# PSUM given out by the list of steps, singly or two banks side by side, in a Performer and Fourier-mixing kernel on one core

## The chip, the core and the metric

The kernel runs on one NeuronCore of a Trainium2 chip. The core has a matrix engine (TensorE, in the profile PE, with its weight loads shown apart as PEld), a vector engine (VectorE, DVE), a scalar engine (ScalarE, ACT), GpSimd (POOL) and a queue engine (SyncE, SP) that here only issues DMAs. Matrix products land in PSUM, eight banks of 512 float32 in each of 128 partitions. The metric is the device time of one execution in microseconds; a kernel's time is the median of several executions.

## The reference

Two blocks follow each other. The first is Performer attention on 8 batches of 8 heads with 576 rows of 64; the second a Fourier mixing with a two-layer perceptron on rows of 512:

```python
def phi(x):
    proj = np.einsum('bhsd,md->bhsm', x, omega)        # 64 -> 128 features
    h = proj - np.sum(x * x, axis=-1, keepdims=True) / 2.0
    h = h - np.max(h, axis=-1, keepdims=True)
    return np.exp(h) / np.sqrt(m)
q_p, k_p = phi(q * scale), phi(k * scale)
kv = einsum('bhsm,bhsd->bhmd', k_p, v); z = np.sum(k_p, axis=2)
x = einsum('bhsm,bhmd->bhsd', q_p, kv) / (einsum('bhsm,bhm->bhs', q_p, z)[..., None] + 1e-06)
# (B,H,S,D) -> (B,S,H*D), then
u = x + real(fft(fft(x, axis=1), axis=2))
un = (u - mean(u)) / sqrt(var(u) + 1e-06)
out = u + maximum(un @ w_ch1, 0.0) @ w_ch2             # 512 -> 2048 -> 512
```

q, k, v and omega are float32; the two weight matrices arrive as float64 and are narrowed on the chip.

## The kernel before

**Two halves.** The early half does attention, the mixing, the narrowing of the weights and the perceptron of four blocks of 128 rows ("plain"). The late half does the perceptron of the other eight blocks of 512 rows with Strassen's seven products (Winograd's form) for both layers: `first_of` for the first layer, `product_of` for the second.

**A list of steps.** The order of instructions on every engine is written out by the program itself. Each stream of work (a Python generator) yields a `Step` ahead of the instructions that it covers: engine or choice of engines, an assumed duration, the events that it needs, the buffers that it takes and gives back, and a `bias` in microseconds that is added to its start when steps are compared. `Listing.run` takes, again and again, the step with the earliest assumed start plus bias, and so fixes the order. A step marked `port` also needs an assumed port that DVE and POOL share; whoever is chosen for it holds that port. The order is then kept as it is; semaphores see to the data. Durations in the list steer the order alone.

**A pair of heads** (`attn(n)`, 32 of them, three under way at once). k and q of two heads are loaded side by side, turned by 9 transposes of 128 columns (line 396) and copied out by ACT. The projection `pairs_of` runs on nine columns of 128: twice four columns as quarters of the array (line 471, 64 by 64, four side by side, results in two banks), and the ninth as one product over the full array (line 461) against a matrix om2 that holds omega twice, with zeros beside it. `softmax` takes one bank at a time: DVE finds the negated maxima (line 412: 512 elements for a bank of a group of four columns, 256 for the ninth), ACT makes one exponential for each 128 (line 424). Then come kv (`kvp`, line 506, two banks, copied out by DVE or ACT in two instructions, lines 521 and 523), 9 transposes of q's features, and numerator and denominator (`ndp`, lines 550 and 558, two banks). Six DVE instructions divide them into x: two additions (571), a reciprocal (574) and three multiplications (581), of which the last covers 64 partitions.

**The mixing** (`mix`, once a batch) folds x on DVE or POOL (608 to 636), multiplies by cosine and sine tables (654, 681, 686), and `residual` adds the parts (700 to 717) and stores them.

**Weights.** 32 pieces of 512 KB are loaded on POOL's queue. For each, `narrow` makes a float32 out of the two halves of the float64: a first scaling on ACT or POOL (lines 333 and 331), four DVE instructions (335, 337, 340, 342) and a sum on POOL (344). After the last one, `w2_parts` makes sums of the second layer's weights (956), and `block_norms(0, ...)` prepares the first late block.

**PSUM.** Eight buffers of one bank come from a pool (`bank(name)`); the list counts free ones under the name "bank". The late half closes the early pools and opens a PSUM pool of its own.

**Late half.** `weight_sums` makes sums of the first layer's weights, 16 DVE instructions (line 1044) into w1s, a tile that lies where early tiles lay; `first_of` needs its first quarter for its second product. `loads_w2` reads pieces of the second layer's weights ahead of need into 15 buffers (line 1137).

## Time and profile before

| | us |
|---|---|
| runs, median of 4 (lowest to highest) | 1237.34 (1235.48 to 1239.09) |
| the profiled execution | 1239.09 |
| its span, first to last instruction | 1237.1 |
| PE busy in the span | 1201.9 |
| DVE busy | 770.2 |
| ACT busy | 456.1 |
| POOL busy | 393.6 |

The granted clock of TensorE was 0.992 in the mean. The early half's last product (line 886) runs until about 475 us and the late half's first one (line 1059) starts at 476.12. Busy time of PE counts every moment in which a product is in flight, so overlapping products are counted once and a busy PE is not yet one at its full rate. In a row of instructions the columns are the line, the engine and operation, the tiles written and read, the shapes and the count, then busy time and mean length in ns, and behind the next bar the engine's idle time ahead of them with what ended it.

### The profile page before, as it was taken

To read this page: it belongs to the slowest core of one execution; us is meant where nothing else is said; L and a number is where in the kernel's file an instruction comes from. 1 tells how busy PE (TensorE), PEld (TensorE's weight loads), DVE (VectorE), ACT (ScalarE), POOL (GpSimd) and SP (SyncE) were. 2 spreads that over 40 slices of the span, in tenths; PEclk is the share of its full clock that TensorE was granted. 3 is DMA by queue.
4 is the path that set the end of the run, shared out by engine and by line. 5 is a ranking of instruction groups with operands and counts; after the bars stand their busy time and mean duration, and the time that the engine had idled before them with its cause. 6 is when DMAs were issued, how large, how long until landed. Compare 5 with 4: busy or idle time off the path is not lost.

```text
span 1237.1 us, 31364 instructions
## 1 busy us (share of the span) xinstructions
PE 1201.9 (97%) x12513; PEld 1073.5 (87%) x12513; DVE 770.2 (62%) x1708; ACT 456.1 (37%) x1430; POOL 393.6 (32%) x462
## 2 busy tenths in 40 slices
PE   7999899999999998999999999999999999999997
PEld 5788878778887875899899899899899899899897
DVE  3999899997687625185185185276276276266265
ACT  5776666676664211222222222222222222222211
POOL 2544354643133110430430530530530530531430
PEclk8999999999999999999999999999999999999999
DMA  8555455646564345078078078078078068068155
GB/s 242 170 170 168 150 156 189 205 120 196 160 206 137 107 145 168 12 258 254 9 251 260 10 240 262 11 235 276 8 224 279 17 212 278 30 198 283 39 159 165
DMA packets 148736, 205.99 MB, mean 167 GB/s; under 512 B 49264, under 2 KB 62320, under 8 KB 148592
## 3 DMA queue, kind: packets, MB, share of 16 engines
q1 hardware_dynamic: 143984, 187.22, 48.2%
q0 software_dynamic: 4608, 16.78, 4.2%
q8 instruction: 99, 1.62, 0.5%
q14 instruction: 45, 0.37, 0.1%
HBM read 172.23 MB, written 35.91 MB: 168 GB/s over the span
## 4 chain that ended last, share of the span: by engine, by line
PE 85%; DVE 9%; ACT 3%; issue 1%; DMA 1%; SPq 0%; DVEq 0%; ACTq 0%
PE sx L1059 17%; PE sx L1204 16%; PE sz L1059 9%; PE sz L1204 8%; PE sy L1059 4%; PE hp L863 4%; PE sy L1204 4%; PE op L886 4%; PE yp L654 4%; PE tps L396 4%; PE pp L471 3%; ACT e L424 2%; PE kvp L506 2%; DVE nmx L412 2%; PE ndp L550 1%
## 5 line engine op out<-in xcount | busy, mean ns | idle before, releaser
L424 ACT ACTIVATE e<-pp,nmx 128x128 f32<-128x128 f32 x576 | 159.3, 407 | 46.4 <-DVE nmx L412 46.2
L1121 POOL TENSOR_TENSOR hs<-hid 128x256 f32<-128x256 f32 x64 | 46.5, 726 | 358.0 <-DVE hid L1047 358.0
L1047 DVE CUSTOM_DVE_ANT_0 hid<-sz,s 128x256 f32<-128x256 f32 x64 | 27.2, 425 | 182.4 <-PE sz L1059 174.5
L1059 PE MATMUL sx<-unT,w 128*128 128x256 f32 x512 | 127.7, 379 | 2.2 <-ACT s L1073 1.4
L1204 PE MATMUL sx<-wl,sums 128*128 128x128 f32 x896 | 115.4, 275 | 0.0
L1204 PE MATMUL sz<-wl,sums 128*128 128x128 f32 x896 | 114.2, 275 | 0.0
L412 DVE TENSOR_REDUCE nmx<-pp 128x4 f32<-128x512 f32 (+1 forms) x160 | 94.2, 628 | 30.8 <-PE pp L471 16.7
L1059 PEld LDWEIGHTS sx<-unT,w 128*128 128x128 f32 x512 | 96.6, 190 | 16.2 <-ACT s L1073 1.8
L1204 PEld LDWEIGHTS sz<-wl,sums 128*128 128x128 f32 x896 | 107.7, 192 | 0.4
L1204 PEld LDWEIGHTS sx<-wl,sums 128*128 128x128 f32 x896 | 107.6, 192 | 0.0
L1073 ACT ACTIVATE s<-sx 128x256 f32<-128x256 f32 x128 | 48.9, 383 | 152.3 <-PE sx L1059 74.3
L344 POOL TENSOR_TENSOR w<-w,raw 128x512 f32<-128x512 f32 x32 | 45.7, 1430 | 120.2 <-DVE raw L342 113.1
L1106 ACT ACTIVATE hid<-sx 128x256 f32<-128x256 f32 x64 | 24.5, 383 | 132.9 <-PE sx L1059 132.9
L471 PE MATMUL pp<-om,kqT 64*64 64x128 f32 x2048 | 71.1, 279 | 0.8 <-issue 0.6
L796 POOL TENSOR_TENSOR rstd<-rstd,mhalf 128x1 f32<-128x1 f32 x36 | 25.3, 702 | 142.9 <-DVE rstd L794 116.2
L471 PEld LDWEIGHTS pp<-om,kqT 64*64 64x64 f32 x2048 | 58.2, 136 | 12.2 <-issue 6.9
L1204 PE MATMUL sx<-wl,hid 128*128 128x128 f32 x512 | 67.6, 275 | 0.0
L863 PE MATMUL hp<-unT,w 128*128 128x128 f32 x512 | 62.2, 276 | 3.8 <-ACT e L424 2.8
L863 PEld LDWEIGHTS hp<-unT,w 128*128 128x128 f32 x512 | 59.5, 192 | 6.2 <-ACT e L424 3.4
L1059 PE MATMUL sx<-tt,w 128*128 128x256 f32 x256 | 64.2, 379 | 0.0
L1182 ACT ACTIVATE s<-sx 128x128 f32<-128x128 f32 x112 | 31.0, 277 | 88.5 <-PE sx L1204 60.7
L1059 PE MATMUL sz<-tt,w1s 128*128 128x256 f32 x256 | 61.9, 379 | 1.7 <-DVE w1s L1044 1.7
(134 smaller groups left out, 2578.5 us busy)
## 6 DMA issues: line engine op xcount, KB each, us to landing
wl<-w2l SPq DMA_DIRECT2D x392, 256.0 KB, 3.8
raw<-in_moe_w_ch_dram POOLq DMA_DIRECT2D x32, 512.0 KB, 4.7
kq<-in_k_dram SPq DMA_DIRECT2D x32, 288.0 KB, 3.6
kq<-in_q_dram SPq DMA_DIRECT2D x32, 288.0 KB, 4.8
vd<-in_v_dram SPq DMA_DIRECT2D x32, 288.0 KB, 4.5
out_dram<-ur SPq DMA_DIRECT2D x72, 128.0 KB, 3.0
u<-us SPq DMA_DIRECT2D x32, 256.0 KB, 4.4
ur<-us SPq DMA_DIRECT2D x32, 256.0 KB, 3.8
```

Of the source, the lines that this page charges most:

```text
L344: nc.gpsimd.tensor_tensor(out=dst, in0=dst, in1=lof, op=ALU.add)
L396: nc.tensor.transpose(ps[:, (j - j0) * 128 : (j - j0 + 1) * 128], src(j), ident[:])
L412: nc.vector.tensor_reduce(nmx[:, 0:num], ps[:, 0 : MF * num].rearrange("p (c m) -> p c m", m=MF), axis=AX.X, op=ALU.max, negate=True,)
L424: nc.scalar.activation(out=e[:, c, :], in_=ps[:, MF * c : MF * c + MF], func=AF.Exp, bias=nmx[:, c : c + 1],)
L471: nc.tensor.matmul(pps[c][cols, MF * m : MF * m + MF], lhsT=kqT[rows, j, cols], rhs=om2[rows, c, :],)
L654: nc.tensor.matmul(yp[:, 0:NK], lhsT=fold[:, c, n, :], rhs=tab[:, c, :], start=(c == 0), stop=(c == NC3 - 1),)
L863: nc.tensor.matmul(hp[:, 0:TP], lhsT=w1[:, dc, 128 * fc : 128 * fc + 128], rhs=unTs[key][:, dc, :], start=(dc == 0), stop=(dc == NDC - 1),)
L886: nc.tensor.matmul(yp[:, 0:DM], lhsT=hs[fc][:, 128 * i : 128 * i + 128], rhs=w2[:, fc, :], start=(fc == 0), stop=(fc == NFC - 1),)
L1059: nc.tensor.matmul(ps[:, 0:HT], lhsT=left(dc), rhs=right(dc), start=start and dc == 0, stop=(dc == D2 - 1), skip_group_check=True,)
L1073: nc.scalar.activation(out=s[:], in_=ps[:, 0:HT], func=AF.Copy)
L1121: nc.gpsimd.tensor_tensor(out=o, in0=l, in1=r, op=op)
L1204: nc.tensor.matmul(ps[:, 0:128], lhsT=left[:, f], rhs=wls[j, i, n][:, f], start=start and f == 0, stop=(f == 3), skip_group_check=True,)
```

## The change

PSUM becomes one tile of eight banks that lives through both halves. The list now keeps a time for each bank: a step takes a "bank" or a "duo", two neighbours that start at an even number, and `got()` hands the chosen banks to the code. A single bank is taken, where times are equal, from a pair that is half in use. What works on two banks at once in the new code: the maxima of a group of columns, the copy of kv, and the division in x. The ninth projection runs on quarters like the others and takes a duo; om2 has omega once. A step marked `port` holds the port only if its engine is DVE or POOL, and the first scaling in `narrow` is such a step, at 1.4 us for POOL where it was 1.0. The middle part of the second fold runs on DVE only. The first quarter of `weight_sums` moves into the early half and writes a tile of its own, with the third sum in that tile rather than in w1; the other three quarters stay. The v load of pair 0 joins the stream of the other v loads instead of following q of pair 0. The wl buffers go from 15 to 14. The memsets of om2 and of x's last rows go. Many biases and some assumed durations get other values.

```diff
+WIDTH = {"bank": 1, "duo": 2}
...
+    def on_port(self, eng):
+        return self.port and eng in (DVE, POOL)
...
+    def banks_at(self, n, t):
+        best = None
+        for i in range(0, 8, n):
+            free = self.banks[i] if n == 1 else max(self.banks[i], self.banks[i + 1])
+            key = (max(free, t), n == 1 and self.banks[i ^ 1] <= t, free, i)
+            if best is None or key < best:
+                best = key
+        return best[3], best[0]
...
-    NWL, NSUM = 15, 3
+    NWL, NSUM = 14, 3
...
-    psum = early.enter_context(tc.tile_pool(name="psum", bufs=8, space=PSUM))
+    psum = ctx.enter_context(tc.tile_pool(name="psum", bufs=1, space=PSUM))
+    banks = psum.tile([128, 8, 512], F32, name="banks")
...
+            yield Step(SP, 0.45, 3.6, makes=("kq", n), kb=288, bias=-2.98)
             nc.sync.dma_start(kq[:, R : 2 * R, :], q[b, h].rearrange(rows, r=R))
-            if n == 0:
-                yield from load_v(0)
...
-        yield Step(SP, 0.6, 4.0, take=(f"vd{n % NV}",), makes=("vd", n), kb=288)
+        yield Step(SP, 0.6, 4.0, take=(f"vd{n % NV}",), makes=("vd", n), kb=500, bias=0.52)
...
-        step = Step({ACT: 0.7, POOL: 1.0}, after=(("raw", i),), bias=0.22)
+        step = Step({ACT: 0.72, POOL: 1.4}, after=(("raw", i),), port=True, bias=1.11)
...
-        yield Step(DVE, 0.15 + 0.135 * num)
-        nmx = small.tile([P, 4], F32, name="nmx", tag="nmx", bufs=4)
+        yield Step(DVE, 0.15 + 0.27 * num, bias=-0.56)
+        nmx = small.tile([P, 2, 4], F32, name="nmx", tag="nmx", bufs=4)
+        pps = psum_of(b)
         nc.vector.tensor_reduce(
-            nmx[:, 0:num],
-            ps[:, 0 : MF * num].rearrange("p (c m) -> p c m", m=MF),
+            nmx[:, :, 0:num],
+            pps[:, :, 0 : MF * num].rearrange("p b (c m) -> p b c m", m=MF),
...
-            if len(ts) == 1:
-                nc.tensor.matmul(
-                    pps[0][:, 0 : 2 * MF],
-                    lhsT=kqT[:, js[0], :],
-                    rhs=om2[:].rearrange("p i m -> p (i m)"),
-                )
+            for m, j in enumerate(js):
+                for c, i in ((0, 0), (1, 1), (0, 1), (1, 0)):
+                    rows, cols = slice(D * c, D * c + D), slice(D * i, D * i + D)
+                    nc.tensor.matmul(
+                        pps[cols, c, MF * m : MF * m + MF],
+                        lhsT=kqT[rows, j, cols],
+                        rhs=om2[rows, :],
+                    )
...
+            if step.eng == DVE:
+                nc.vector.tensor_copy(out=kv[:], in_=kvp[:, :, 0 : D + 1])
+            else:
+                nc.scalar.activation(out=kv[:], in_=kvp[:, :, 0 : D + 1], func=AF.Copy)
...
+        nc.vector.tensor_scalar(rden[:], nd[:, :, :, D], DEN_EPS, None, op0=ALU.add)
         nc.vector.reciprocal(out=rden[:], in_=rden[:])
+        dst = x[:, :, 2 * D * pr : 2 * D * (pr + 1)].rearrange("p c (i d) -> p i c d", i=2)
+        nc.vector.tensor_tensor(
+            out=dst,
+            in0=nd[:, :, :, 0:D],
+            in1=rden[:].unsqueeze(3).to_broadcast([P, 2, 5, D]),
+            op=ALU.mult,
+        )
...
-            step = Step({DVE: 1.15, POOL: 2.5} if n else DVE, 1.15, port=True)
+            yield Step(DVE, 1.15, port=True, bias=-0.08)
...
+    w1s = [const.tile([128, 4, D2, GW], F32, name="w1s0")]
+    def weight_sums(groups):
+        yield Step(NONE, after=("converted",))
+        for g in groups:
...
+                if g == 0 and i == 2:
+                    o = w1s[0][:, 3]
...
-        + [w2_parts(), block_norms(0, mlpp), plain(), weights()]
+        + [w2_parts(), weight_sums((0,)), block_norms(0, mlpp), plain(), weights()]
...
-    psum = ctx.enter_context(tc.tile_pool(name="psum2", bufs=8, space=PSUM))
...
-    listing.run([late_norms(), halves(), loads_w2(), weight_sums()])
+    listing.run([late_norms(), halves(), loads_w2(), weight_sums((1, 2, 3))])
```

## The prediction

> **What bounds the kernel now.** I read the busy shares and the forty slices first, then the stretches of the early half, then the rows by shape, last the timeline where the halves meet. The page first:

> ```profile
> PE 1201.9 (97%) x12513; PEld 1073.5 (87%) x12513; DVE 770.2 (62%) x1708; ACT 456.1 (37%) x1430; POOL 393.6 (32%) x462
> ...
> PE   7999899999999998999999999999999999999997
> ...
> DVE  3999899997687625185185185276276276266265
> ```

> The reader should distrust the 62% of DVE: it is an average. From slice 2 to slice 9 DVE is as full as PE; from slice 17 on it is mostly free and PE alone is full. The change edits the first half, so that half is read by stretches (columns: PE, PEld, DVE, ACT, POOL busy, then clock, DMA share, GB/s):

> ```profile
> 31.00:279.00 248.00, 235.92 (x4428) 197.99 (x4417) 233.89 (x552) 170.98 (x573) 116.99 (x105) 0.99 0.55 165
> 279.00:403.00 124.00, 120.28 (x2224) 102.01 (x2223) 93.73 (x251) 76.64 (x253) 34.54 (x31) 1.00 0.56 174
> 403.00:475.00 72.00, 72.00 (x411) 52.33 (x409) 28.78 (x67) 13.98 (x43) 8.00 (x10) 1.00 0.32 108
> 475.00:500.00 25.00, 21.09 (x95) 17.70 (x95) 14.39 (x26) 5.00 (x14) 7.25 (x11) 1.00 0.63 211
> 0.00:31.00 31.00, 22.30 (x425) 18.06 (x428) 11.68 (x27) 17.75 (x57) 7.41 (x19) 0.89 0.83 242
> ```

> Between 31 and 279 us DVE works 233.9 of 248 us and PE 235.9. But PE's busy time holds overlaps: taking each matmul at its start-to-next-start time inside an unbroken group (0.112 us for 128 columns in full mode, 0.029 for a projection quarter, 0.429 for 512 columns) its work there is 207 us, so PE loses 41 us to waits and to changes of array shape, while DVE has 14 us left. DVE is the tighter of two tight engines. Between 279 and 403 the same sum gives PE 112 of 124; from 403 to 475 it has no gap at all, and behind 500 the slices show 9 throughout. So the change can earn before 403 and at the seam near 476, and nowhere else.

> **DVE over two banks.** The rows by shape, and one back-to-back series from the timeline (start, length):

> ```profile
> L412 DVE TENSOR_REDUCE nmx<-pp 128x4 f32<-128x512 f32 x128 | 82.3, 681 | 26.5 <-PE pp L471 16.7 <-ACT e L424 9.0 <-issue 0.6
> ...
> L581 DVE TENSOR_TENSOR x<-ndp,rden 128x256 f32<-128x256 f32 x64 | 24.2, 419 | 1.1
> ...
> L412 DVE TENSOR_REDUCE nmx<-pp 128x2 f32<-128x256 f32 x32 | 13.3, 416 | 4.3 <-ACT e L424 3.7 <-PE pp L461 0.4
> ```
> ```profile
> 113.97 2.46 DVE L412 TENSOR_REDUCE nmx<-pp 128x4 f32<-128x512 f32 x4
> ```

> The price of a reduction is not its 681 ns: four take 2.46 us, (2.46 - 0.68)/3 = 0.59 apart. The slope between the two shapes is (681-416)/256 = 1.035 ns an element, so 512 elements are 0.530 and what is paid per instruction is 0.068 us. Merging saves that and no element. Per pair of heads: two reductions go (four of 512 become two of 1024; the ninth stays one of 256), two of the three multiplications (256+256+128 becomes 640), one of the two additions into rden, and one copy of kv where DVE makes it (32 of 64 copies, so 0.5). That is 5.5 x 0.068 = 0.37 us, x 20 pairs (60 rows of L581 in that stretch, three a pair) = **7.5 us** of 233.9, and 11 pairs x 0.37 = 4 us up to 403, where DVE has room and it buys nothing. [...]

> **Conversion, port and POOL.** The weight conversion's three DVE lines are stretched:

> ```profile
> L335 DVE TENSOR_SCALAR raw<-raw x32: 407/422/1592, 28.9 to 264.9; 128x512 uint32<-128x512 uint32 x32
> L337 DVE SCALAR_TENSOR_TENSOR w<-w,raw x32: 673/682/1671, 29.4 to 274.7; 128x512 uint32<-128x512 uint32 x32
> L340 DVE TENSOR_SCALAR raw<-w x32: 427/429/1662, 30.1 to 275.4; 128x512 uint32<-128x512 uint32 x32
> ```

> In the stretch they take 20.35, 26.30 and 19.01 us for 31 each, 18.5 us above 31 medians. Their long ones are as long as a POOL operation (L331: 1.55), so DVE waits for POOL. The edit makes the list price L331 at 1.4 instead of 1.0 us on POOL, against 0.72 on ACT. ACT has 77 us idle in the stretch, so I take 12 of the 25 to move: 19 of POOL's 117 us, 16% of 18.5 = 3 us off DVE, for 8.5 us more on ACT. Ends: 0 (none move) and 18.5 (the new port order ends every clash). The middle fold now stays on DVE: POOL took one of 16, so DVE gains about 1.2 us of work. Net **2 us**; DVE in sum 9.5.

> **The ninth projection.** Line 461 takes 0.432 us at best from its start to the next group's, 0.536 in the median, because it lies in full mode beside quarters. A quarter group of four columns takes 0.924, so one is 0.231. Gain 0.20 to 0.31, I take 0.25: 5 us over 20 pairs, 2.9 over the 11 or 12 left. The new form has four maxima rather than two in that instruction, over the same 256 elements, and no more exponentials.

> Between 31 and 279 DVE falls by 9.5 and PE by 5; both are tight, so the stretch shrinks by something between: **7.5**. From 279 to 403 PE sets the pace: **2.5** of its 2.9.

> **The seam.** Columns: start, length, engine, then in brackets the idle time before and its releaser:

> ```profile
> 476.12 1.97 PE L1059 MATMUL sx<-unT,w 128*128 128x256 f32 x8 [0.87 <-DVE ur L899]
> 478.99 0.69 DVE L1044 TENSOR_TENSOR w1s<-w 128x512 f32<-128x512 f32 x1 [3.01 <-DMA out_dram<-ur]
> ...
> 479.78 1.97 PE L1059 MATMUL sz<-tt,w1s 128*128 128x256 f32 x8 [1.69 <-DVE w1s L1044]
> ...
> 490.00 1.13 PE L1059 MATMUL sx<-unT,w 128*128 128x256 f32 x4 [1.35 <-ACT s L1073]
> ```

> PE waits 0.87 for the old PSUM pool, 1.69 for sums that may not start until the last store has landed (their tile lies where the early tiles lay), and 1.35 behind sixteen sums on DVE. One PSUM tile ends the first; the first quarter of the sums, now made early in a tile of its own, ends the second: PE then has six products of 0.864 us to do before it needs a saved one, past 479.1. The third shrinks, twelve sums for sixteen ending 2.4 us sooner. I take **3.3** of 3.9; ends 0.9 and 3.9. The four sums moved forward, 4 x 0.60 us on DVE, fall after the last conversion (291), where DVE is idle 30 of 124 us; uncovered they would cost 2.4.

> **The start.** PE sits 4.33 us until the second kq lands at 15.2. The v load of pair 0 is no longer ahead of it on SP (0.69 us of issue, 288 KB), and the four weight loads that share the DMA still go at 2.7. I take **1.5**, ends -1 (the v load lands too late for the first kvp at 20.4) and 4.3. The memsets removed are 1.3 us of POOL beside the first loads.

> **Edits at nothing.** One wl buffer fewer: a load is issued 14 leaves before its use, 14 x 0.893 = 12.5 us, and lands after 3.8 (at most 7.2), so SP's wait for the freed buffer stays hidden; with no cover every leaf would be late. Biases reorder the list; no row prices an order, so I bound it by 8 us either way, under half of the 18.6 us that the list of waits gives PE's weight loads from 31 to 279 apart from "issue".

> Sum: 7.5 + 2.5 + 3.3 + 1.5 = 14.8. The profiled execution, span 1237.1 and 1239.09 in all, would be 1222.3 and 1224.3; the median shown, 1237.34, lies 1.75 below that execution, so **1222.5**.

> **Rivals.** *Paired banks stall PE (slower).* A pair must be free in both halves and be aligned; the ninth group takes two banks instead of one; and the first half of each big pair waits 1.13 us for its maximum instead of 0.60. [...] For it: hp and pp read nothing that ACT's e writes, so where they wait on "ACT e" they wait for a bank; and eight banks make four pairs, while each pair of heads asks for five in turn, with three pairs of heads under way. Against: all waits on "ACT e" between 31 and 279, those for data too, are 5.4 us of PE's and 11.1 of its weight loads'. If two thirds of the two longer holds (2 x 0.53 us) reach PE, that is 0.7 us x 32 = 22 us: 1222.5 + 22 = 1244.5. It decides from 14.8/32 = 0.46 us a pair.

> *DVE's gain is hidden.* PE's losses are shape changes (a group's median is 0.05 to 0.16 above its best), not DVE. Then the ninth projection's surest part, 0.20 us x 31 = 6.2, and the seam's surest, 0.9, are all: 7.1 us, 1230.2. For it: the chain of waits is 85% PE and 9% DVE. Against: DVE's 94%.

> *The port clears.* Nearly all of the 18.5 us and the 7.5 come through, PE's 41 us of losses give the room: 7.5 + 15 + 2.5 + 3.3 + 1.5 = 30, 1207.5. Against: POOL's sums L344 and L716 stay.

> **Chances.** Forecast 0.46 (its own range 1214 to 1229), hidden 0.17, port 0.15, paired banks 0.22. Within 0.2%, 2.5 us, which is about what this measurement can tell, falls 0.07, out of the hidden case and the mild paired one. Faster 0.74, slower 0.19. The range 1205 to 1240 leaves out the worse part of the paired case and the best of the port case.

> **What would show it.** Right: L412 at 64 rows of 128x1024 near 1.21 us and 32 near 0.42; L581 at 32 near 0.73; DVE from 31 to 270 under 95%; more than five conversions on ACT; no L1044 ahead of the first sz, and the seam near 464. Wrong: new PE waits on "ACT e" or "DVE nmx" ahead of pp, kvp and ndp, DVE idle growing in the same stretch, or a slice below 9 behind the seam.

## The result and the profile after

The changed kernel takes **1232.3 us** (median of 40 runs, 1228.3 to 1238.2) beside 1236.8 for the kernel before (61 runs, 1232.7 to 1240.7): ratio 0.9963, 95% interval 0.9956 to 0.9970, or **4.6 us saved** where 14.8 were forecast. The profiled spans are 1230.8 and 1237.1 us, 6.3 apart. The page of the kernel after, busy shares and two rows of slices:

```profile
PE 1191.0 (97%) x12705; PEld 1066.0 (87%) x12705; DVE 745.2 (61%) x1519; ACT 458.7 (37%) x1434; POOL 384.9 (31%) x451
...
PE   6879899999999999999999999999999999999997
...
DVE  4889899887677643285285275276276266267255
```

The stretches (PE, PEld, DVE, ACT, POOL busy, then clock, DMA share, GB/s):

```profile
0.00:31.00 31.00, 21.61 (x491) 18.47 (x495) 12.40 (x19) 20.32 (x64) 8.15 (x18) 1.00 0.96 263
31.00:279.00 248.00, 227.94 (x4585) 193.02 (x4574) 220.13 (x436) 178.30 (x573) 106.70 (x99) 0.99 0.55 164
279.00:403.00 124.00, 124.00 (x2121) 103.39 (x2123) 88.56 (x184) 72.78 (x241) 20.29 (x18) 1.00 0.58 185
...
470.00:500.00 30.00, 27.75 (x121) 24.17 (x122) 12.39 (x24) 6.85 (x19) 10.60 (x15) 0.94 0.47 165
```

The reader is to set two numbers of the second row beside those of before. DVE fell from 233.9 to 220.1 us, more than the 9.5 forecast. PE's busy time fell too, from 235.9 to 227.9: **DVE's saving turned into idle time on DVE, and PE waits more.** (8.0 us less of PE's busy time is more than the 4.0 that the shorter ninth projection takes off in this stretch.) In PE's row of the page the second and third slices (31 to 92 us) are 8 and 7, where both were 9; the 8 of the old seam is gone. By busy time, the conversion's three stretched lines give 9.4 us of DVE's fall in this stretch, the maxima 5.3, the division 2.4, the folds 2.1 and the copies of kv 2.3: DVE makes 6 of the 32 copies now, where it made 32 of 64, so most of that is work handed to ACT, which the forecast had not in it. The groups by shape (busy us, mean ns, idle before):

```profile
L459 DVE TENSOR_REDUCE nmx<-banks 128x8 f32<-128x1024 f32 x64 | 78.0, 1219 | 37.7 <-PE banks L515 35.5 <-ACT e L476 2.0
L612 DVE TENSOR_TENSOR x<-banks,rden 128x640 f32<-128x640 f32 x32 | 26.4, 825 | 1.1
...
L459 DVE TENSOR_REDUCE nmx<-banks 128x2 f32<-128x256 f32 x32 | 13.3, 416 | 2.9 <-ACT e L476 1.5 <-ACT kv L565 1.4
```

64 maxima at 1219 ns and 32 at 416 are as foreseen, and 82.3 us fell to 78.0, 0.067 for each merged pair. The division takes 825 ns where 730 were forecast, yet 26.4 us in all beside 32.9 before. The conversion, in the tile's own view (min, median and max ns, first and last start):

```profile
L382 DVE TENSOR_SCALAR raw<-raw x32: 406/420/1051, 28.2 to 273.1; 128x512 uint32<-128x512 uint32 x32
L384 DVE SCALAR_TENSOR_TENSOR w<-w,raw x32: 672/684/818, 28.6 to 273.6; 128x512 uint32<-128x512 uint32 x32
L387 DVE TENSOR_SCALAR raw<-w x32: 428/430/1425, 29.4 to 274.3; 128x512 uint32<-128x512 uint32 x32
...
L378 POOL TENSOR_SCALAR w<-raw x18: 1521/1542/1773, 10.4 to 252.7; 128x512 f32<-128x512 f32 x18
L380 ACT ACTIVATE w<-raw x14: 667/696/813, 25.2 to 270.5; 128x512 f32<-128x512 f32 x14
```

ACT does 14 of the 32 scalings where it did 5, and the three stretched DVE lines together fell from 67.2 to 57.8 us of busy time (L387 alone rose, from 19.4 to 22.1).

**Where the time went.** A busy PE says nothing of progress, so I added up PE's work (each matmul at its start-to-next-start time in an unbroken group) by stretch, and took into account that the ninth projection on quarters is 0.20 us less of that work for each of the 32 pairs of heads:

| part of the span | forecast, us | in the two traces, us |
|---|---|---|
| start, to 31 us | -1.5 | -2.1 (0.6 of it the ninth's) |
| 31 to 279 | -7.5 | **+0.8** |
| 279 to 403 | -2.5 | -6.9 |
| 403 to the end of the early products | 0 | +0.8 |
| seam | -3.3 | **+0.2** |
| last matmul to the end | 0 | +0.85 |
| sum | -14.8 | -6.35 (spans: -6.3) |

The last early product ends at 467.7 us where it ended at 475.1, 7.4 earlier. The clock has a share in these rows: the trace before has two steps of 3.413 us at half clock from 13.5 to 20.3 us and two between 31 and 279, the trace after one between 31 and 279 and one at the seam, and a step costs up to 1.7 us of PE's work (last section). The tail grew from 6.68 to 7.53 us: SP issues the last eight stores in 5.0 us in both kernels, but starts them 0.55 us ahead of the last matmul's end where it started 1.4 ahead.

### The profile page after: what moved, and what is told of

It is laid out like the page before. It is cut to its first block, busy times and chain, and to the rows that moved or that the text cites. A ratio compares the mean times of both kernels' runs of the same rounds, so it can differ in the third digit from the quotient of the medians.

```text
span 1230.8 us, 31634 instructions
## 1 busy us (share of the span) xinstructions
PE 1191.0 (97%) x12705; PEld 1066.0 (87%) x12705; DVE 745.2 (61%) x1519; ACT 458.7 (37%) x1434; POOL 384.9 (31%) x451
## 4 chain that ended last, share of the span: by engine, by line
PE 91%; DVE 5%; ACT 2%; issue 1%; DMA 1%; SPq 0%; DVEq 0%; ACTq 0%
PE banks L1099 31%; PE banks L1252 29%; PE banks L917 5%; PE banks L894 5%; PE banks L515 4%; PE banks L441 4%; PE banks L683 4%; PE banks L549 3%; PE banks L592 2%; PE banks L710 2%; ACT e L476 2%; DVE nmx L459 2%; PE banks L833 1%; PE banks L715 1%; DVE raw L387 1%
## 5 line engine op out<-in xcount | busy, mean ns | idle before, releaser
L1252 PE MATMUL banks<-wl,sums 128*128 128x128 f32 x1792 | 220.3, 275 | 0.0
L1252 PEld LDWEIGHTS banks<-wl,sums 128*128 128x128 f32 x1792 | 210.5, 192 | 1.0
L476 ACT ACTIVATE e<-banks,nmx 128x128 f32<-128x128 f32 x576 | 160.0, 395 | 36.6 <-DVE nmx L459 36.4
L1099 PE MATMUL banks<-unT,w 128*128 128x256 f32 x704 | 167.3, 379 | 0.0
L1099 PEld LDWEIGHTS banks<-unT,w 128*128 128x128 f32 x704 | 132.7, 190 | 17.9 <-issue 0.5
L1099 PE MATMUL banks<-tt,w1s 128*128 128x256 f32 x512 | 127.5, 381 | 2.7 <-ACT s L1113 2.7
L459 DVE TENSOR_REDUCE nmx<-banks 128x8 f32<-128x1024 f32 (+1 forms) x96 | 88.1, 952 | 40.6 <-PE banks L515 35.5
L1099 PEld LDWEIGHTS banks<-tt,w1s 128*128 128x128 f32 x512 | 97.7, 191 | 16.4 <-ACT s L1113 3.1
L1252 PE MATMUL banks<-wl,hid 128*128 128x128 f32 x768 | 98.8, 275 | 0.0
L1252 PEld LDWEIGHTS banks<-wl,hid 128*128 128x128 f32 x768 | 94.0, 192 | 1.2
L515 PE MATMUL banks<-om,kqT 64*64 64x128 f32 x2304 | 77.9, 279 | 4.2 <-ACT kqT L448 2.6
L515 PEld LDWEIGHTS banks<-om,kqT 64*64 64x64 f32 x2304 | 64.9, 136 | 16.0 <-issue 5.5
```

Of the source, the lines that this page charges most:

```text
L459: nc.vector.tensor_reduce(nmx[:, :, 0:num], pps[:, :, 0 : MF * num].rearrange("p b (c m) -> p b c m", m=MF), axis=AX.X, op=ALU.max, negate ...
L476: nc.scalar.activation(out=e[:, c + (i if num == 1 else 0), :], in_=pps[:, i, MF * c : MF * c + MF], func=AF.Exp, bias=nmx[:, i, c : c + 1],)
L515: nc.tensor.matmul(pps[cols, c, MF * m : MF * m + MF], lhsT=kqT[rows, j, cols], rhs=om2[rows, :],)
L1099: nc.tensor.matmul(ps[:, 0:HT], lhsT=left(dc), rhs=right(dc), start=start and dc == 0, stop=(dc == D2 - 1), skip_group_check=True,)
L1252: nc.tensor.matmul(ps[:, 0:128], lhsT=left[:, f], rhs=wls[j, i, n][:, f], start=start and f == 0, stop=(f == 3), skip_group_check=True,)
```

## The experiments

My theory was that the maxima over two banks delay the exponentials, that PE waits for these and for the banks they hold, and that this ate the gain. The rivals: DVE's time was never the bound, so nothing came of its saving; the seam lost the rest; or the order of the list, fitted anew by the biases, decides over all of it. Each kernel below is the changed one with one edit unless said otherwise. "Against the changed kernel" is the difference of the two ratios to the kernel before, times 1236.8 us.

**1. One maximum for each bank, first bank first.**

```diff
-        nc.vector.tensor_reduce(nmx[:, :, 0:num], pps[:, :, 0 : MF * num]...)
+        for w in (0, 1):
+            nc.vector.tensor_reduce(nmx[:, w, 0:num], pps[:, w, 0 : MF * num]...)
```

> Only edit: each two-bank maximum of the changed kernel is made as two instructions of one bank, the first bank first; the list and its order stay. DVE gets 96 more instructions x 0.068 us = 6.5 us, some 60 of them (4 us) between 31 and 279 us. If DVE's work still sets the pace there (theory A), the time is 3 to 4 us over the changed kernel (1232.3), about 1236. If PE's waits for results, not DVE's work, set it (theory B: latency), the first four exponentials can start 0.53 us sooner after each big projection and the time is the same or up to 5 us lower, 1228 to 1232.

1227.1 us (5 runs), ratio 0.9927 (0.9914 to 0.9940): **4.5 us faster** than the changed kernel, with intervals that do not meet, although DVE has more to do: 96 instructions and 5 us of busy time.

**2. The same, second bank first** (`for w in (1, 0)`). Same instructions, but the exponentials still begin with the first bank, so their first maximum comes as late as with one instruction over both.

> As split_first, but the second bank's maximum is made first, so the exponentials of the first bank, which stand first in ACT's order, wait as long as for one instruction over both banks. Theory A (DVE's work): 3 to 4 us over the changed kernel, as split_first. Theory B (latency): within 1.5 us of the changed kernel, and slower than split_first by what the early start is worth.

1236.4 us (12 runs), ratio 0.9998 (0.9986 to 1.0010). Only the order of the two maxima differs between 1 and 2, which moves the first one that ACT needs by 0.6 us, and the times lie **9 us** apart. Against the changed kernel run 2 is 4.3 us slower, which the latency theory (within 1.5 us) did not foresee: here the 96 extra instructions of DVE cost what theory A said, 3 to 4 us. The stretches of 1 and then of 2, columns as above:

```profile
31.00:279.00 248.00, 231.09 (x4629) 194.96 (x4620) 227.06 (x503) 179.63 (x577) 110.59 (x101) 0.99 0.56 168
```
```profile
31.00:279.00 248.00, 229.92 (x4550) 195.07 (x4541) 217.73 (x480) 175.86 (x568) 105.08 (x95) 0.96 0.55 164
```

In the same 248 us the first gets through 79 more matmuls, and the granted clock is 0.99 against 0.96: part of the cost of a late exponential comes by way of the clock (last section). These two executions overstate it: run 2's is the slowest of its twelve (1239.9 us), with six steps of 3.413 us at half clock in this stretch beside one in run 1's. DVE is busier where the kernel is faster. PE's waits up to 480 us, first the changed kernel's, then those of 1 (us in total, times, longest):

```profile
PE banks L441 <- ACT e L476: 6.8, 7, 1.9
PE banks L549 <- ACT e L476: 4.0, 5, 1.4
...
PE banks L1099 <- ACT s L1113: 2.7, 1, 2.7
PE banks L515 <- ACT kqT L448: 2.6, 4, 0.8
PE banks L592 <- ACT e L476: 2.0, 1, 2.0
```
```profile
PE banks L550 <- ACT e L477: 3.6, 5, 1.1
PE banks L516 <- ACT kqT L448: 3.4, 5, 1.4
PE banks L441 <- ACT e L477: 3.3, 3, 1.3
```

L441 is the line of all transposes, of kq and of q's features e. By the tiles that it reads, 6.65 of the changed kernel's 6.8 us stand ahead of transposes of kq. These read nothing of e: where they wait on "ACT e", they wait for a **bank** that the exponentials have not released. Before the change the line named 1.5 us,

```profile
PE tps L396 <- ACT e L424: 1.5, 4, 0.5
```

and all of it ahead of transposes of e itself; bank waits on "ACT e" stood then ahead of hp (2.8 us). In run 1 the kq transposes wait 3.3 us, half of what they do in the changed kernel, and in run 2 7.7. L549 (L550) is kvp, which reads e; L592 is ndp.

**3. Maxima in pieces of two columns** (256 elements): 8.7 us more of DVE instructions than in 1 at 0.068 each, 7.4 more of its busy time in the traces.

> split_first carried on: each maximum covers 256 elements, four instructions for a big group, in the same order; the ninth's stays two of 128. DVE gets 128 more than split_first x 0.068 = 8.7 us, the first exponential can start 0.27 us sooner than there. If the gain of split_first is the start of the exponentials, half as much again less DVE's count comes out: -2.5 + 4 (by split_second's +4 for 6.5 us of DVE), 1228 to 1230, over split_first and under the changed kernel. If the earlier start is all, 1224 to 1225; if only the half-length hold of the first bank counted, over 1231.

1231.1 us (5 runs), ratio 0.9954 (0.9941 to 0.9966), 3.3 us slower than 1 and just past the 1228 to 1230 forecast. A still earlier first maximum did not pay for the longer DVE work. If the 3.3 us are DVE's 8.7, a us of it costs 0.4 here; but the clock can have made them as well (last section), so this price is not shown.

**4. The other two-bank operations taken apart** (kv's copy and the addition into rden twice, three multiplications).

> Only edit: the copy of kv, the additions into rden and the multiplications into x are made bank by bank again (two, two and three instructions); the maxima stay over two banks, the list and its order stay. DVE and, for kv, ACT get 0.24 us more a pair of heads, 5 us between 31 and 279 us. Theory B (latency of results that PE waits for): ndp's two banks come free and x is ready at the same end plus 0.2 us, kv's end is 0.07 to 0.13 us later, and PE waits for kv and banks only now and then, so +1 to +3 us over the changed kernel (1232.3). Theory A (DVE's count): +4 to +5. A gain would say that merging costs here as it does for the maxima.

1233.2 us (11 runs), ratio 0.9979 (0.9966 to 0.9991): **2.0 us slower** by the ratios, but the intervals meet, and the early half ends at 467.6 us in its trace, as in the changed kernel's (467.7). A small gain from merging these, as theory B has it (1 to 3 us), fits but is not settled; a cost like that of the maxima is not seen.

**5. The ninth projection in full mode again**, with omega twice as it was, in one bank of its pair.

```diff
+            if len(js) == 1:
+                nc.tensor.matmul(pps[:, 0, 0 : 2 * MF], lhsT=kqT[:, js[0], :],
+                                 rhs=om3[:].rearrange("p i m -> p (i m)"))
-            for m, j in enumerate(js):
+            for m, j in enumerate(js if len(js) > 1 else ()):
```

> Only edit: the ninth projection is one product over the full array again (256 columns into the first bank of its pair), with its maximum and exponentials read from there; the list keeps its order. If the quarters are what the change earned (theory B: PE's time and its changes of shape), the time rises by 0.20 to 0.31 us x 32 = 6.4 to 10 us, to 1238.5 to 1242, and is then slower than the kernel before. If the gain came from DVE (theory A), PE has room between 31 and 279 us and the time rises by 2 to 4 us.

1239.8 us (11 runs), ratio 1.0028 (1.0016 to 1.0040): **8.0 us slower**, 0.25 us for each of 32 pairs. Without this part the change would be a loss. The row (busy us, mean ns) is the old one again:

```profile
L520 PE MATMUL banks<-om,kqT 128*128 128x256 f32 x64 | 23.1, 443 | 0.6 <-DVE x L625 0.6
```

**6. The seam.** The timeline of the changed kernel (start, length, engine; in brackets the idle time before and its releaser):

```profile
467.67 1.03 PE L1099 MATMUL banks<-unT,w 128*128 128x256 f32 x4
...
468.54 1.03 PE L1099 MATMUL banks<-tt,w1s 128*128 128x256 f32 x4
468.59 1.15 SPq L810 DMA_DIRECT2D out_dram<-ur  x2
...
471.81 0.66 ACT L1113 ACTIVATE s<-banks 128x256 f32<-128x256 f32 x2 [13.59 <-DMA out_dram<-ur]
...
472.25 2.04 PE L1099 MATMUL banks<-tt,w1s 128*128 128x256 f32 x4 [2.69 <-ACT s L1113]
...
474.08 2.71 PE L1099 MATMUL banks<-unT,w1s 128*128 128x256 f32 x8
```

Two products run early as foreseen. Then the list puts the third, which needs a first product saved, before the products that need nothing; and the place to save it is free only when the last early store has landed, at 471.8. PE stands for 2.69 us, and then four matmuls take 2.04 us and eight 2.71 which take 1.03 and 1.89 a little later: the clock has halved, to a granted 0.50 from 472.3 to 475.7 us. The edit tells the list that the saved products' buffers are free later:

```diff
+    listing.buffers["s"] = [listing.free[PE] + 3.4] * 6
```

> Only edit: the list is told that the six s buffers come free 3.4 us after PE's last early step, so that it puts four to five products ahead of the first one that needs a saved one, where the changed kernel has two. Theory: the seam lost 2.7 us of PE to the wait for s plus 1.7 us to the 3.4 us of half clock that follow in its trace. If the low clock follows from the wait, the time falls by 3 to 4.4 us, to about 1228.5; if it would come anyway, by 1.5 to 2.5; if the lost time returns later because DVE's sums hold up the products next, by less than 1.

1230.0 us (6 runs), ratio 0.9953 (0.9939 to 0.9967), 1.2 us less than the changed kernel and less than the 3 to 4.4 foreseen; the intervals meet, so alone this is not settled. The timeline shows the edit at work:

```profile
468.96 1.03 PE L1100 MATMUL banks<-unT,w 128*128 128x256 f32 x4
469.83 1.03 PE L1100 MATMUL banks<-tt,w1s 128*128 128x256 f32 x4
470.69 1.03 PE L1100 MATMUL banks<-unT,w 128*128 128x256 f32 x4
471.55 1.03 PE L1100 MATMUL banks<-tt,w1s 128*128 128x256 f32 x4
473.56 1.99 PE L1100 MATMUL banks<-tt,w1s 128*128 128x256 f32 x8 [0.98 <-ACT s L1114]
```

Four products come first, and of the loss at the seam 1.55 us (1.14 and 0.41) are left of 4.6. Its profiled execution shows little of that in its span (1230.5 us beside 1230.8), as its early half ended 1.3 us later, with four steps at half clock in it where the changed kernel's has one.

**7. Edits 1 and 6 together.**

> split_first and seam_late together: maxima bank by bank, and four products ahead of the first that needs a saved one. If the two gains are apart in place they add: 1227.1 - 1.2 = about 1226; if split_first already got rid of the seam's half clock by itself (its trace has none there), the seam gives only its shorter wait, and 1226 to 1227 comes out either way.

**1226.0 us** (4 runs, 1225.3 to 1227.1), ratio 0.9919 (0.9905 to 0.9932): the fastest kernel of the study, 5.4 us under the changed one, about the sum of the two, and not clear of run 1, whose interval it overlaps.

**8. The price list of the scaling as it was**, to send the conversions back to POOL: `Step({ACT: 0.7, POOL: 1.0}, ..., bias=0.22)`, no port step.

> Only edit: the first scaling in narrow is priced for the list as in the kernel before (ACT 0.7 or POOL 1.0, no port, bias 0.22), so that the list gives most of the 32 to POOL again; the rest of the list follows from that. If the move to ACT (14 of 32, 5 before) and the port took stretch off DVE as its three conversion lines show (58.9 us after, 67.2 before), the time rises by 2 to 4 us over the changed kernel. If ACT's extra work delays exponentials as much as it helps DVE, the time is within 2 us either way; an order that no longer fits its biases could cost more, which would show in PE's waits.

1247.0 us (6 runs), ratio 1.0094 (1.0077 to 1.0111). This run missed its aim: ACT still got 17 of the 32, so it says nothing on the port, and yet it lost 16.2 us. So I asked what an order is worth.

**9. One bias alone**, that of the scaling, 1.11 to 0.22.

> Only edit: the bias of narrow's first step is 0.22 instead of 1.11, prices stay. narrow_old changed price, port and this bias together and came out 15 us over the changed kernel. If the order's fit made that, this lands 5 to 15 us over it as well, 1237 to 1247, though nothing computed or priced is other than in the changed kernel; if price and port made it, this stays within 2 us of 1232.

1253.7 us (4 runs), ratio 1.0141 (1.0126 to 1.0157): **22 us slower**, beyond the 5 to 15 foreseen, with not one instruction more. But a bias also moves work between engines: in this trace ACT makes 28 of the 32 scalings, where it made 14, besides 6 more copies for the perceptron (line 880) and 7 fewer of kv. So the run does not part the order from ACT's load, which delays the exponentials too. Its waits of PE up to 540 us:

```profile
PE banks L515 <- ACT e L476: 6.0, 4, 4.0
PE banks L894 <- ACT e L476: 5.1, 3, 3.4
PE banks L549 <- ACT e L476: 5.0, 7, 2.2
PE banks L441 <- ACT e L476: 4.8, 7, 1.2
```

L515, L894 and L441's transposes of kq (3.5 of its 4.8 us) read no e; they wait for banks, 14.5 us in all.

**10 and 11. No biases at all**, in the changed kernel and in the kernel before (the list's key is `got[0]` alone).

> The changed kernel with every bias in its list ignored; all other instructions, prices and buffers stay. With its counterpart, the kernel before without biases, it tells how much of either time is the fitted order. Theory: an order that is not fitted costs 10 to 25 us in both (narrow_old and before_ninth lost 15 and 31 against what their edits should bring), so 1242 to 1257.

> The kernel before with every bias in its list ignored. If the change's structure alone (quarters, merged division, fewer instructions) is worth the 5 us that undoing its parts showed, this is about 5 us slower than after_nobias; if banks in pairs only work because the biases were fitted to them, it is faster than after_nobias.

1302.3 us and 1261.3 us (4 runs each), ratios 1.0532 (1.0511 to 1.0553) and 1.0203 (1.0188 to 1.0217). The kernel before loses 25 us without its biases, the changed one 70; unfitted, the new scheme is the slower by 41, far more than the 10 to 25 us foreseen for both. That is the outcome set down for pairs of banks that work only with biases fitted to them. But here too engines change with the order, DVE makes 24 copies of kv in run 10 where it made 6, so the pairs alone are not shown to be the cause. PE's waits on "ACT e" up to 540 us are 26.1 and 16.7 us in these two, 13.2 in the changed kernel and 6.1 in the kernel before. About 14 of the 70 us were lost in the late half, where there is no e.

**12. The kernel before with the ninth projection on quarters** in two of its single banks, the biases left as they were.

> The kernel before with only the ninth projection changed: quarters into two banks, two maxima of 128 elements and two exponentials, in the list 0.24 us in quarters and two banks. Theory B: the quarters are the gain, PE loses 0.20 to 0.31 us x 32, so 1237 - 6 to 10 = 1227 to 1231, less 0.068 x 32 = 2 us of DVE for the second maximum, 1229 to 1232. If the second bank that it takes costs PE waits (theory C, bank pressure), the gain is under 3 us.

1261.7 us (4 runs), ratio 1.0200 (1.0180 to 1.0219). The same part that is worth 8 us in the changed kernel seems to cost 25 here. After 9 I do not take this for a measurement of the part: its biases were fitted to other instructions. Its own rival, that the second bank makes PE wait, is not excluded either: PE's waits on "ACT e" ahead of rows that read no e are 12.2 us up to 540 us here, 3.4 in the kernel before.

## Why the prediction was wrong

Faster was right, the size was not: 4.6 us for 14.8. The time lies inside the range of 1205 to 1240, but over the forecast's own 1214 to 1229.

**The step that failed is "both are tight, so the stretch shrinks by something between: 7.5".** It took two full engines for two bounds, and most of DVE's saved time for time of the kernel. From 31 to 279 us DVE worked 13.8 us less and PE was 0.8 us behind. What the runs showed: merging the maxima has two effects of opposite sign. The 96 instructions saved are worth 4.3 us (run 2 against the changed kernel); the later start of the exponentials costs 8.8 (run 2 against run 1), as the first one of a large group starts 0.53 us later (1219 ns for 684), PE waits for e, and the banks come free later. The forecast had the first and put nothing for the second; in sum the merged maxima lose 4.5. The rest of DVE's saving did not show in this stretch either: in run 1's trace, with the maxima apart, PE is 3.1 us ahead of the kernel before there, and the ninth projection alone makes up 4.2. Why it did not, though the conversion alone took 9.4 us off DVE there, was not tested and stays open.

- **Ninth projection: right**, in mechanism and size. 5 and 2.9 us were forecast, 8.0 were measured (run 5). It stands for more than the whole gain. The instruction still makes two maxima (128x2), though, not four.
- **Paired banks, the rival: right in mechanism, wrong in size.** It named the later first exponential and the waits on "ACT e" by rows that read no e. It put 0.7 us a pair of heads on the longer waits; 8.8 / 32 = 0.28 came, less than the 0.46 from which it would have decided alone. The forecast should have carried it as a cost. That each maximum keeps to one bank does not by itself explain the gain of run 1: run 2 does so too, and it is 4.3 us slower than the changed kernel. What it costs that pairs must be aligned and free in both halves was not tried apart from the order and stays open.
- **Conversion and port: right in kind, low in size.** 9 scalings went to ACT, not 12, and the three lines lost 9.4 us rather than 3. How little it bought in its stretch is said above; the one run meant to price it (8) missed its aim. The rival "The port clears" needed nearly all of it to come through.
- **DVE's gain hidden, the rival: nearest by number** (1230.2, at a chance of 0.17). Its surest part, the ninth projection, is what the gain rests on. Its reason is not the whole: run 2 shows that DVE's instructions do cost time, and the seam gave nothing in sum. The signs set down for being wrong came: new waits of PE on "ACT e", and more idle time on DVE.
- **Seam: wrong.** "PE then has six products to do before it needs a saved one" counted six products that depend on nothing, and did not read which the list would take. It took two. The forecast gain of 3.3 became 0.2 of loss, with 1.7 us of half clock in it; run 6's trace shows the products' order as the cause, for 3.0 of the 4.6 us; in its time 1.2 came, not clear of the noise.
- **279 to 403: too low**, 6.9 for 2.5. 3.1 us of it match waits ahead of kvp in the trace before, for which the profile names no cause ("issue"), and which the trace after does not have. The conversions end at 283 us instead of 293, which frees DVE earlier; whether that earned anything was not tested.
- **Start: right by number, by luck.** 1.5 were forecast from a shorter wait for the second kq. That wait of 4.33 us is gone, but others stand in its place: PE is idle for 5.2 us before and 5.3 after, from its first transpose to 21 us. What differs is the clock: before, PE worked 5.0 us at half clock between 13.5 and 20.3 us, which is 2.5 us of work lost, and after none. So the first kvp starts at 16.7 us rather than 20.4. **Tail: missed**, 0.85 us.
- **Biases "at nothing", 8 us either way: probably too narrow.** One of them moves 22 us, by order and choice of engine together (run 9). How much of the change's 4.6 us is new biases cannot be had from these runs.

In parts, by what undoing each costs: ninth -8.0, divisions and copies -2.0 (not settled), maxima +4.5, all else (start, seam, tail, conversion, order) +0.9 as the remainder: -4.6. That the parts add was not tested.

## What to carry to other kernels

Before an instruction is merged with its neighbour, ask who waits for its first half: a merged maximum saved 0.07 us on its engine and held up the first exponential by 0.53, a merged division held up nobody that the runs show. A busy share of 94% on a second engine is no proof that its time is the kernel's time; take its work away in one place and see whether the first engine's work is done sooner. Where a fitted order of instructions lies behind both kernels, an edit that leaves the order unfitted measures the order, and the engines it chooses, along with the edit: compare edits that change it little, and distrust the rest.

## What the runs showed of the hardware

| PE idle in a step of 3.413 us | steps | next step at half clock |
|---|---|---|
| 1.88 us or more | 37 | 37 |
| 1.60 to 1.88 | 26 | 9 |
| under 1.60 | 2177 | 14, 9 of them behind a step already at half |

In the trace before, the granted clock changes at 13.47, 20.30, 40.78, 44.19, 146.59 and 150.01 us, which are 2, 6, 1, 30 and 1 steps of 3.413 us apart, and it is 0.50 in the stretches that begin with the first, third and fifth of these. A step in which PE was idle for 1.88 us, 55% of it, was enough in all 37 cases. So the same wait of 2.7 us at the seam halves the clock in one kernel's trace and not in another's, as the grid cuts it: in the changed kernel one step held all 2.69 us, in run 1 two steps held 1.05 and 1.65; in runs 5 and 4 the fullest held 1.82 and 1.81, and in these three the clock stayed.

A step at half clock costs PE, if it is busy throughout, half of 3.413, or 1.7 us of work. Take one minus the mean granted clock, times the time, as what an execution lost by its clock (given to 0.001, which is 1.2 us). Over 41 executions of the changed kernel, with clocks from 0.989 to 0.997, the time rises by 0.92 us for each us so lost, with a correlation of 0.82. The median loss is 6.2 us before, 7.4 after, 3.7 in run 1, 8.7 in run 2 and 7.4 in run 3. By this estimate some 5 of the 9 us between runs 1 and 2 came through the clock, 3.7 of the 4.5 between run 1 and the changed kernel, and perhaps all of the 3.3 between runs 1 and 3. The wait counts by itself too: in the traces of run 1 and of the changed kernel, each with one such step between 31 and 279 us, PE does 4.0 us more of work there in run 1. How the 4.5 us part between wait and clock stays open. **Waits of about 2 us, each small by itself, cost up to 1.7 us more where they fall into one step of that grid**, and a late exponential makes such waits.
